# Linear attention and gated MLP on one core: which transfers SyncE waits for before the program ends

## The chip, the core and the metric

The kernel runs on one core of a Trainium2 chip. The core has five instruction streams: TensorE (PE) multiplies matrices, VectorE (DVE) and ScalarE (ACT) work on elements, GpSimd (POOL) does small set-up work and issues accumulating transfers, and SyncE (SP) computes nothing: here it issues nearly all DMA transfers and waits for semaphores. A semaphore is a counter that an instruction or a finished transfer raises; a wait holds an engine's own stream until the counter has reached a value.

The metric is the device time of one execution in microseconds; the median over the timed runs counts. Beside them stands one profiled execution. Its "span" runs from the first to the last instruction that the profile has of the program.

## The reference

`x` is 2048 x 1024, in bf16. It is normalised per row, and the result `xn` goes two ways: through linear attention with 32 heads (A), and through a gated MLP with 3584 inner columns (B). The output joins them.

```python
xn = _layernorm(x, axis=-1)
# A: qkv = xn @ wqkv, per head of 32 columns
pq, pk = phi(q), phi(k)                  # phi(t) = where(t > 0, t + 1, exp(t)) + 1e-6
kv  = einsum("bhsd,bhse->bhde", pk, v);  z = sum of pk over s
o   = einsum("bhqd,bhde->bhqe", pq, kv) / (einsum("bhqd,bhd->bhq", pq, z) + 1e-6)
s   = o @ wo
# B
g   = _silu((silu(xn @ w_gate) * (xn @ w_up)) @ w_down)
return x + s * g
```

## The kernel before

**Tiling and stages.** The large products are made block-wise with seven partial products for each 2 x 2 blocks in place of eight (class `Set`), with sums and differences of blocks formed by VectorE and ScalarE; some of the seven are split once more in the same way (class `Joint`). The stages are: normalise `x` and transpose it; K and V and their sums over rows; gate, up and Q for column blocks of 512; the attention output `s`, which goes to a scratch tensor in DRAM (`s_scr`); at the end the product with `w_down`.

**The last stage.** It runs over four groups `g` of 512 rows (class `Group`). The function `evac` inside `Group.dset` finishes a piece of the output: ScalarE takes the silu of a finished PSUM bank, VectorE multiplies it with the piece of `s`. In groups 0 to 2, GpSimd adds the piece to the output in DRAM by an accumulating transfer (helper `dacc`, L374). In group 3, VectorE adds `x`, which was loaded for it, and SyncE stores the piece (helper `dma`, L370). The semaphores of these stores are named `d_oo`, then the number of the buffer for `x` (0 to 7), then the first column. Buffer 7 is stored in three pieces, of 256, 128 and 128 columns (`PIECES`), so there are ten of them, and each is raised by one transfer.

**What sets the order.** Every operation is recorded by `Plan.op` with the tile regions that it reads and writes. From those regions `op` works out `preds`, the earlier operations that it must wait for, and `succs`, the later ones that must wait for it. `Plan.schedule` simulates the five streams and settles one order for each; the list `BOOST` of hand-set preferences bears on it. `Plan.emit` walks that order and writes, for each engine, a list of entries `("w", semaphore, value)` for a wait and `("i", function, semaphore, increment)` for an operation. A wait is left out where the engine knows already, by an earlier wait of its own or through the engine it waited for, that the semaphore has reached the value. `o.ev` holds an operation's semaphore, the key of it, the value that it reaches with the operation, and what the engine knew by then. `PL.count` holds each semaphore's final value. `_run` (L219) plays an engine's list: L222 is `wait_ge`, the next lines the operation.

**The end of the program.** After `emit`, waits are appended to SyncE's list. They stand behind its last store, and no operation of SyncE follows them. Then SyncE leaves its block by a branch and takes part in the barrier of all engines that ends the program (both have the line L254 in the profile). The compiler puts up to two waits into one semaphore instruction, and the last wait into the branch.

Of the kernel before, what the change touches and what calls it, by code (L numbers as in the profile page):

```python
# [240 lines left out]
def build_kernel(nc, A_x, A_wqkv, A_wo, B_w_gate, B_w_up, B_w_down, out, WINDOW=10, NWARM=13, NPE=4, LEAD=16.0, CLAMP=1000.0, AHEAD=4.0):  # L241
# [12 lines left out]
    with ExitStack() as es:  # L254
# [76 lines left out]
        semn = {}  # L331
# [6 lines left out]
        PL = Plan(WINDOW, LEAD, CLAMP, AHEAD)  # L338
# [1300 lines left out]
        sp = {}  # L1639
# [99 lines left out]
            PL.ops[k].boost = v  # L1739
        PL.schedule()  # L1740
        prog = PL.emit(esem)
        for s in semn.values():
            if id(s) in PL.count:
                prog["sp"].append(("w", s, PL.count[id(s)]))

        @block.tensor
        def _(h):
# [19 lines left out]
def bass_recurrent_scan__linear_attn_block__swiglu_ffn__prompt_kernel(  # L1767
    nc: bass.Bass,
    A_x: bass.AP,
    A_wqkv: bass.AP,  # L1770
    A_wo: bass.AP,
    B_x: bass.AP,
    B_w_gate: bass.AP,
    B_w_up: bass.AP,
    B_w_down: bass.AP,
    out: bass.AP,
):
    build_kernel(nc, A_x, A_wqkv, A_wo, B_w_gate, B_w_up, B_w_down, out)
# [28 lines left out]
```

## Time and profile before

| | before |
|---|---|
| timed runs, median (lowest to highest) | 705.55 us (705.12 to 705.91), 3 runs |
| profiled execution, its own time | 704.51 us |
| span of the profiled execution | 702.7 us |
| granted TensorE clock, mean | 0.998 |
| last matmul ends | 696.75 us |
| SyncE's semaphore instructions of L222: all / from 698 us on | 69 / 59 |

In the rows that follow, "start us, us" are the start from the beginning of the span and the time that it took. SPq, POOLq and so on are instructions of an engine's sequencer alone (waits, barriers, branches, DMA issues); the profile doesn't count them as busy, and the chain of waits doesn't run through them unless something counted was released. In the views by source line, "x59: 17/28/28, 698.4 to 702.2" is the count, the shortest, median and longest duration in ns, and the first and last start. A row that begins with two times and a colon is a stage of the table by stage: it has the length, the busy time of PE, PEld, DVE, ACT and POOL, the granted clock, the mean busy share of the 16 DMA engines and GB/s. A row "DMA" with 40 digits has the busy share of the DMA engines in tenths, in 40 equal slices of the stretch. In a row of a DMA issue the last number is the time from issue to landing.

### The profile page before, as it was taken

Reading aid. Unit: us, or ns where it says so; the run is one execution under the profiler, and the core shown is the slowest. Engines: PE = TensorE matmul, PEld = TensorE weight load, DVE = VectorE, ACT = ScalarE, POOL = GpSimd, SP = SyncE. Lnnn points to the kernel's source line nnn. Section 1 sums busy time; section 2 is a strip of 40 time slices with the busy share of each in tenths; the row PEclk is TensorE's granted clock in tenths of the full one; section 3 lists DMA queues with packets and bytes.
Section 4 is the critical chain, followed back from the end, with each engine's and each line's share of the span. In section 5 each row is a group of like instructions: output and inputs, shape, how many; then the busy total and the mean of one; then the engine's idle time right before and its main releaser. Section 6 shows DMA issues by size and latency. Waiting matters only on the chain.

```text
span 702.7 us, 11996 instructions
## 1 busy us (share of the span) xinstructions
PE 694.8 (99%) x4436; PEld 421.4 (60%) x4436; DVE 610.7 (87%) x1391; ACT 424.7 (60%) x848; POOL 68.4 (10%) x87
## 2 busy tenths in 40 slices
PE   8999999999999999999999999999999999999996
PEld 3544445555555566666666666666665448687784
DVE  6999998667999799898999999888879998768685
ACT  4877645867978967868866567775763113232222
POOL 2111000001100011020110110001101211111010
PEclk9999999999999999999999999999999999999999
DMA  9434213126612376584670486766627875666672
GB/s 313 106 83 106 54 60 121 61 90 145 155 61 69 117 195 169 174 236 101 166 194 1 106 242 198 242 218 165 165 81 225 192 182 176 155 165 156 207 180 69
DMA packets 96107, 103.68 MB, mean 148 GB/s; under 512 B 18256, under 2 KB 91344, under 8 KB 95952
## 3 DMA queue, kind: packets, MB, share of 16 engines
q1 hardware_dynamic: 84976, 92.43, 41.9%
q0 software_dynamic: 11072, 10.49, 11.9%
q8 instruction: 35, 0.57, 0.3%
q14 instruction: 24, 0.20, 0.1%
HBM read 65.54 MB, written 37.36 MB: 146 GB/s over the span
## 4 chain that ended last, share of the span: by engine, by line
PE 99%; ACT 0%; POOL 0%; DVE 0%; issue 0%; POOLq 0%
PE ps L230 99%; PE ps L237 0%; ACT X L358 0%; DVE W L368 0%; POOL TM L415 0%; ACT W L358 0%; POOL TM L414 0%; POOLq L1792 0%
## 5 line engine op out<-in xcount | busy, mean ns | idle before, releaser
L358 ACT ACTIVATE TM<-ps 128x512 f32<-128x512 f32 (+2 forms) x341 | 169.0, 528 | 50.5 <-PE ps L230 45.6
L368 DVE TENSOR_TENSOR ps<-ps,TM 128x256 f32<-128x256 f32 (+1 forms) x322 | 157.7, 509 | 40.2 <-PE ps L230 35.8
L230 PE MATMUL ps<-X,W 128*128 128x512 f16 (+1 forms) x896 | 190.4, 340 | 0.0
L230 PE MATMUL ps<-P,W 128*128 128x512 f16 (+1 forms) x896 | 188.9, 338 | 0.0
L358 ACT ACTIVATE H<-ps 128x512 f16<-128x512 f32 (+1 forms) x181 | 106.3, 601 | 55.9 <-PE ps L230 54.9
L230 PEld LDWEIGHTS ps<-X,W 128*128 128x128 f16 (+1 forms) x896 | 87.5, 98 | 59.5 <-DVE W L368 0.2
L230 PEld LDWEIGHTS ps<-P,W 128*128 128x128 f16 (+1 forms) x896 | 87.6, 98 | 58.4 <-DVE ps L368 0.2
L358 ACT ACTIVATE ps<-ps 128x256 f32<-128x256 f32 (+2 forms) x149 | 63.5, 426 | 72.5 <-PE ps L230 70.9
L230 PE MATMUL ps<-H,X 128*128 128x512 bf16 (+4 forms) x556 | 104.8, 336 | 0.5 <-ACT X L358 0.5
L368 DVE TENSOR_TENSOR H<-H 128x1024 f16<-128x1024 f16 (+5 forms) x150 | 87.1, 598 | 10.6 <-ACT H L358 8.4
L368 DVE TENSOR_TENSOR W<-W 128x256 f16<-128x256 bf16 (+6 forms) x256 | 89.1, 388 | 5.1 <-PE ps L230 2.9
L230 PE MATMUL ps<-W 128*128 128x256 f16 x512 | 90.0, 273 | 0.0
L368 DVE TENSOR_TENSOR TM<-ps,TM 128x512 f32<-128x512 f32 x99 | 67.8, 686 | 12.5 <-PE ps L230 11.5
L230 PEld LDWEIGHTS ps<-H,X 128*128 128x128 f16 x556 | 52.8, 98 | 41.6 <-ACT X L358 0.6
L375 POOL DMA_DIRECT2D h_scratch<-H x28 | 33.7, 1283 | 437.4 <-DVE H L368 197.0
L230 PEld LDWEIGHTS ps<-W 128*128 128x128 f16 (+1 forms) x512 | 50.0, 98 | 27.3 <-ACT TM L358 0.6
L230 PE MATMUL ps<-H,W 128*128 128x512 f16 (+2 forms) x280 | 63.6, 358 | 0.0
L230 PE MATMUL ps<-H 128*128 128x256 f16 (+4 forms) x432 | 60.9, 273 | 0.0
L230 PE MATMUL ps<-W,H 128*128 128x256 f16 (+1 forms) x314 | 53.5, 305 | 0.0
L358 ACT ACTIVATE H<-TM 128x512 f16<-128x512 f32 x61 | 38.3, 631 | 15.6 <-DVE TM L368 15.0
L230 PEld LDWEIGHTS ps<-H 128*128 128x128 f16 (+1 forms) x432 | 38.3, 98 | 14.6 <-ACT H L358 0.2
L368 DVE TENSOR_TENSOR H<-ps,TM 128x512 f16<-128x512 f32 (+1 forms) x59 | 40.3, 685 | 2.7 <-PE ps L230 2.5
(92 smaller groups left out, 552.1 us busy)
## 6 DMA issues: line engine op xcount, KB each, us to landing
h_scratch<-H SPq DMA_DIRECT2D x70, 256.0 KB, 3.2
X<-h_scratch SPq DMA_DIRECT2D x15, 896.0 KB, 5.2
W<-in_B_w_gate_dram SPq DMA_DIRECT2D x7, 1024.0 KB, 5.4
W<-in_B_w_up_dram SPq DMA_DIRECT2D x7, 1024.0 KB, 6.1
h_scratch<-H POOLq DMA_DIRECT2D x28, 256.0 KB, 5.7
H<-in_B_w_down_dram SPq DMA_DIRECT2D x8, 896.0 KB, 6.7
W<-in_A_x_dram SPq DMA_DIRECT2D x16, 256.0 KB, 3.1
H<-in_A_wqkv_dram SPq DMA_DIRECT2D x8, 512.0 KB, 7.9
```

The costliest lines, as they stand in the source:

```text
L230: last = h.matmul(o, l, r, start=st, stop=sp, skip_group_check=True)
L358: op = PL.op("act", reads, writes, lambda h: h.activation(o, i, func, **kw), nel(o) / 1200.0 + (0.055 if src == "ps" else 0.095))
L368: return dve(reads, writes, lambda h: h.tensor_tensor(o, a, b, op), nel(o), 1.92 if fast else 0.96)
L375: return PL.op("pool", reads, writes, lambda h: h.dma_start(o, i, accum_op=ALU.add), 1.0, sem=s, nbytes=2 * nbytes)
```

## The change

Before, SyncE waits at the end for the final value of every semaphore that any transfer raises: 118 of them. The change goes over the operations in scheduled order and, for each transfer that no later operation depends on (`o.succs` is empty), notes its semaphore with the value that it reaches with that transfer; a later transfer on the same semaphore takes the place of the earlier. Only these are waited for.

```diff
         PL.schedule()
         prog = PL.emit(esem)
-        for s in semn.values():
-            if id(s) in PL.count:
-                prog["sp"].append(("w", s, PL.count[id(s)]))
+        ends = {}
+        for o in PL.order:
+            if o.sem is not None and not o.succs:
+                ends.pop(id(o.sem), None)
+                ends[id(o.sem)] = o.ev
+        for s, _, val, _ in ends.values():
+            prog["sp"].append(("w", s, val))
```

The ten that are left are the stores of group 3. Their order in the list changes too: it is that of the stores now.

The only place where the instructions differ is the end of SyncE's stream. The rows are SyncE's last two stores and the branch out of its block, with the semaphores waited for ahead of it (the row of before is cut off by the view; `s_dve` is VectorE's own semaphore, the `d_` names are those of transfers).

```order
@@ -223,3 +223,3 @@
 L371 DMA out_dram<-W 128x256 [waits s_dve]
 L371 DMA out_dram<-W 128x128 [waits s_dve] x2
-L254 UNCONDITIONAL_BRANCH [waits d_so3,d_so4,d_so2,d_so5,d_so1,d_so6,d_so0,d_so7,d_ha4_1,d_so8,d_hs6_1,d_wdR010,d_hs6_0,d_wdR011,d_ha4_0,d_wdR110,d_ha0_1,d_wdR111,d_hs2_1,d_wdR000,d_hs2_0,d_wdR001,d_ha0_0,d_wdR100,d_rr1_3,d_wdR101,d_rr1_2,
+L254 UNCONDITIONAL_BRANCH [waits d_oo4_0,d_oo6_0,d_oo5_0,d_oo7_0,d_oo2_0,d_oo7_256,d_oo3_0,d_oo7_384,d_oo1_0,d_oo0_0]
```

Nothing ahead of the branch has moved, on SyncE or on the other engines, but for line numbers.

## The prediction

> **What bounds the kernel now.** I read the page first, then the chain of waits in order of time near the end, then the last microseconds stage by stage, and last the waiting instructions themselves, by source line. The page and the end of the chain:
>
> ```profile
> PE 694.8 (99%) x4436; PEld 421.4 (60%) x4436; DVE 610.7 (87%) x1391; ACT 424.7 (60%) x848; POOL 68.4 (10%) x87
> ...
> 679.91 16.84 PE ps L230 x125
> 696.75 0.02 issue
> 696.77 0.28 ACT W L358
> 697.06 0.02 issue
> 697.08 0.24 DVE W L368
> 697.32 0.02 issue
> 697.34 0.23 DVE W L368
> ```
>
> TensorE is busy for 99% of the span, and the chain is TensorE's until 696.75 us; two short evacuations follow, on ScalarE and VectorE. The chain stops there, at 697.57, because the profile does not count semaphore and DMA-issuing instructions as work. The span is 702.7 us, so 5.1 us lie behind the last arithmetic. Nothing of this change stands earlier than that, and these 5.1 us have a limit of their own. The timeline of SyncE, the table by stage, and the transfers from 697.8 us on (40 slices of 0.13 us) show who is at work in them:
>
> ```profile
> 691.41 6.89 SPq L371 DMA_DIRECT2D out_dram<-W  x7
> ...
> 698.30:699.40 1.10, 0.00 (x0) 0.00 (x0) 0.00 (x0) 0.00 (x0) 0.00 (x0) 1.00 0.27 60
> 699.40:702.30 2.90, 0.00 (x0) 0.00 (x0) 0.00 (x0) 0.00 (x0) 0.00 (x0) 0.54 0.01 3
> 702.30:702.70 0.40, 0.00 (x0) 0.00 (x0) 0.00 (x0) 0.00 (x0) 0.00 (x0) 0.50 0.00 0
> ...
> DMA  3940740181000000000000000002000000000000
> q1 hardware_dynamic: 438, 0.14, 10.4%
> q14 instruction: 1, 0.01, 0.6%
> ```
>
> SyncE issues its last store until 691.41 + 6.89 = 698.30. From then on no engine computes (five times 0.00). Up to 699.4 the stores still move, 60 GB/s; from 699.4 to 702.3 the DMA engines are 1% busy. The row of slices says the same: data until the tenth slice, 699.1 us, and one lone digit at slice 28, which starts at 701.3 us and must be the only packet that is not of queue q1, an instruction fetch. So for 2.9 us neither an engine nor a store is busy. What runs is SyncE's list of waits (the helper at L222 issues them):
>
> ```profile
> L222 SPq EVENT_SEMAPHORE  x59: 17/28/28, 698.4 to 702.2; - x59
> ...
> L222 SPq EVENT_SEMAPHORE  x17: 28/28/28, 699.0 to 700.0; - x17
> ...
> L222 SPq EVENT_SEMAPHORE  x1: 28/28/28, 700.4 to 700.4; - x1
> L222 SPq EVENT_SEMAPHORE  x4: 28/28/28, 700.8 to 701.0; - x4
> ...
> L254 SPq COMPARE_BRANCH  x1: 41/41/41, 702.3 to 702.3; - x1
> L254 SPq DRAIN  x1: 7/7/7, 702.5 to 702.5; - x1
> L254 POOLq EVENT_SEMAPHORE  x2: 17/17/17, 702.5 to 702.6; - x2
> ```
>
> The first row is the whole list: 59 instructions, the first at 698.4, the last at 702.2, none longer than 28 ns, so none of them stood waiting. The second is the list between 699 and 700 us: 17 in a microsecond, 0.06 us each. The next two are the list from 700.4 to 700.7 and from 700.7 to 701: there is one pause, from 700.4 to 700.8, some 0.3 us longer than a step. Check: 58 steps of 0.06 plus 0.3 is 3.8 us, as from 698.4 to 702.2. The last rows are the way out: a branch at 702.3, SyncE's drain, the barrier through GpSimd (its own end comes at 702.7). **The end of the program is set by the number of instructions in this list.**
>
> **The change part by part.** It takes 108 of 118 semaphores out of that list. Two semaphores fit one instruction (59 instructions and the branch, with two in 58 of them, carry 118); ten take five instructions and the branch. So 54 of SyncE's instructions go. No other engine's work, no transfer and no order changes; SyncE's last issue stays at 698.30.
>
> *What is removed.* 54 x 0.06 = 3.2 us, plus the pause of 0.3 us, if it belongs to the long list: 3.5 us. By instructions alone the list would end at 698.4 + 5 x 0.06 = 698.7.
>
> *What is late next.* The ten that stay are the output stores themselves, and the last of these is still under way then. The two last stores, and the time from their issue to their landing:
>
> ```profile
> L371 SPq DMA_DIRECT2D out_dram<-W x2: 430/431/432, 697.4 to 697.9; - x2
> DMA to landing us min/median/max: 1.5/1.5/1.5
> ...
> out_dram<-W SPq DMA_DIRECT2D x1, 64.0 KB, 2.0
> out_dram<-W SPq DMA_DIRECT2D x2, 32.0 KB, 1.5
> ```
>
> The last store, 32 KB, is issued at 697.9 and lands 1.5 us later, at 699.4. The one before it lands at 697.4 + 1.5 = 698.9 and the 64 KB one before that 2.0 us after its issue, which is still earlier than 699.4. So of the four real waits only the last counts. It takes back 699.4 - 698.7 = 0.7 us of the 3.5; under those 0.7 us the five remaining wait instructions cost nothing. Without that cover (a landing at once) they would cost 0.3 us. That a SyncE instruction which really waits starts late after the landing is not seen in this list. I bound it below by nothing and above by one step of the list, 0.06 us, and take nothing.
>
> *What stays.* From the last wait (702.2) to the end (702.7): 0.5 us, unchanged.
>
> *The sum.* 699.4 + 0.5 = 699.9 us against 702.7: **2.8 us less in the span.** The profiled execution took 704.5 us, 1.8 us more than its span; I leave those 1.8 us as they are, since they lie outside the program: 701.7 for a profiled run. The median of the timed runs, 705.55, is 1.0 us over the profiled execution, with a spread of 705.1 to 705.9. The difference is taken over: 705.55 - 2.8 = **702.7 us**.
>
> *Bounds.* The landing is the one term that can move: 1.5 us here, 2.0 us for the 64 KB store; the longest for a store of the last stage is this:
>
> ```profile
> L371 SPq DMA_DIRECT2D out_dram<-W x8: 332/332/600, 685.8 to 696.8; - x8
> ...
> DMA to landing us min/median/max: 1.7/1.7/3.0
> ```
>
> With 2.0 for the last store the gain is 2.3 us (703.2), with 3.0 it is 1.3 (704.2). I take 1.5, since it belongs to both stores of that very size at that very place. On the other side a landing of 1.4 with rounding in favour gives 2.9 to 3.0.
>
> **The rivals.**
>
> *Instruction fetch.* A list that is 54 instructions shorter moves every place where SyncE's stream goes on to the next block of instructions. The profile shows one such place: the pause at 700.4, and 0.9 to 1.0 us behind it the fetch of q14, which lasts 0.6% x 16 engines x 5.2 us = 0.5 us. In before that fetch was for instructions that were needed later, so only 0.3 us of it showed. That place is (702.3 - 700.8) / 0.06 = 25 instructions before the branch; with 54 fewer it is 29 behind the branch, in the closing code. If the code behind it is not on hand, SyncE stands for 1.0 + 0.5 = 1.5 us: 2.8 - 1.5 leaves 1.3, 704.3 us. The Trainium skill, Runtime: NRT & Kernel Launch, in Instruction fetch mechanics, speaks for this rival: a taken branch to a target outside the two pages on hand forces a fetch before execution can go on. Against it stand the branch at 702.3 and the drain at 702.5 in before: 0.2 us in all, no room for a fetch, and what follows the branch follows it in the stream too. 3%, for one or two such fetches (two: 705.8).
>
> *Slower.* The same mechanism, in series: the place is the way out behind the branch at L254, the price 1.5 us for each block that has to be fetched with SyncE standing, and every other engine held by the barrier. It decides from the third block on: 3 x 1.5 - 2.8 = 1.7 us lost, 707.2 us. For it speaks only that the border between two blocks moves into the closing code; against it, that the one crossing the trace shows cost 0.3 us and not 1.5. 3%.
>
> *The list is faster without the profiler.* The step of 0.06 us is seen while each instruction is recorded. Elsewhere recorded instructions start closer together, four on GpSimd at the very start:
>
> ```profile
> 0.30 0.10 POOL L1792 MEMSET const-float32-0.0<- 128x1 f32 x1 [0.30 <-issue]
> 0.34 0.10 POOL L1792 MEMSET const-float32-1.0<- 128x1 f32 x1
> 0.37 0.10 POOL L1792 MEMSET const-bfloat16-1.0<- 128x1 bf16 x1
> 0.41 0.10 POOL L1792 MEMSET const-uint8-127<- 128x1 uint8 x1
> ```
>
> (0.41 - 0.30) / 3 = 0.037 us. If that were the step in a timed run, the list of before would end at 698.4 + 59 x 0.037 = 700.6 instead of 702.2, and the change would be worth 700.6 - 699.4 = 1.2 us: 704.4 us. Against it: the recording does not hold the engines to 0.06, as these very rows show, so the step is rather that of the instruction; and the profiled execution was not the slower one. 4%.
>
> *It does nothing.* Something else could set the end, in the 1.8 us outside the span or by a transfer that a dropped wait was really for. The 1% of the DMA engines from 699.4 on, which is the fetch alone, rules out the transfer; a fixed time outside can't be seen from here. 705.5 us, 3%.
>
> **How the numbers follow.** The forecast holds 87%, and the predicted time is its own: 702.7. Its bounds are the landing (2.3 to 2.9 us of gain, 702.6 to 703.2) and the scatter of a median, for which I take the 0.4 us by which the runs of before differ from theirs: 702.2 to 703.6. I widen that by a little at both ends, to **702.1 to 703.9**, for a landing between 2.0 and 3.0 us; the four rivals, 13%, stay outside. 0.2% of the time is 1.4 us; that is about what a measurement of this kernel tells from no change. The forecast is a gain of 2.8 us or 0.4%, so its 87% go to faster. The single or double fetch (3%), the faster list (4%) and no effect (3%) end within 0.2%: 10%. The fetches in series go to slower: 3%.
>
> **What would show it.** Right: in the changed kernel's profile the L222 rows of SyncE behind 698 us fall from 59 to 5 and the last of them starts at 699.4, at the landing of the last store; the branch follows within 0.1 us and the span ends 0.5 us after the landing, at 699.9; no pause is in the list, and the row of slices has no stretch of zeros before the end but the last half microsecond. The chain up to 697.57 is unchanged. Wrong: a gap of a microsecond or more between branch and drain with a q14 packet in it (fetch); a last landing well beyond 1.5 us after its issue (the landing mis-sized); a span that falls by 2.8 while the timed median falls by 1.2 or less (the list faster without the profiler, or a fixed end outside the span).

## The result, and the profile after

| | before | with the change |
|---|---|---|
| timed side by side, median (lowest to highest) | 705.25 us (704.91 to 705.91), 6 runs | 701.84 us (701.15 to 703.17), 6 runs |
| profiled execution, own time | 704.51 us | 701.97 us |
| span of it | 702.7 us | 700.3 us |

The ratio is 0.9954, with a 95% interval of 0.9942 to 0.9966: 3.4 us or 0.5% faster, by the interval 2.4 to 4.1 us. The prediction was faster, 702.7 us, in a range of 702.1 to 703.9. The sign and the mechanism came out; the time lies 0.3 us below the range.

In the changed kernel's profile the end of the chain of waits reads (start us, us, what):

```profile
690.53 6.84 PE ps L230 x62
697.37 0.02 issue
697.39 0.29 ACT W L358
697.68 0.02 issue
697.71 0.24 DVE W L368
697.94 0.02 issue
697.97 0.22 DVE W L368
```

The links are those of before, but each is 0.6 us later (697.97 in place of 697.34). The change can't do that; where it comes from is told below. Behind it, the views by source line once more: the waits, the last store, the way out.

```profile
L222 SPq EVENT_SEMAPHORE  x5: 17/28/28, 698.7 to 699.8; - x5
...
L371 SPq DMA_DIRECT2D out_dram<-W x1: 433/433/433, 698.2 to 698.2; - x1
DMA to landing us min/median/max: 1.5/1.5/1.5
...
L254 SPq COMPARE_BRANCH  x1: 41/41/41, 699.9 to 699.9; - x1
L254 SPq DRAIN  x1: 7/7/7, 700.0 to 700.0; - x1
```

And the table by stage for the same stretch (from, to and length, then five engines' busy time, the granted clock, the DMA engines' share and GB/s):

```profile
699.10:699.80 0.70, 0.00 (x0) 0.00 (x0) 0.00 (x0) 0.00 (x0) 0.00 (x0) 1.00 0.21 47
699.80:700.30 0.50, 0.00 (x0) 0.00 (x0) 0.00 (x0) 0.00 (x0) 0.00 (x0) 0.95 0.00 0
```

The 59 wait instructions are 5. The last store is issued at 698.2 and lands 1.5 us later, at 699.8 (698.23 + 1.55 by its unrounded times); the last wait starts then, the branch 0.1 us behind it, and the span ends 0.5 us after the landing. Stores move until 699.8, and only the last half microsecond is empty. From the start of the last issue to the end it is 700.3 - 698.2 = **2.0 us**, in before 702.7 - 697.9 = **4.8 us**. (By the unrounded times 2.02 and 4.83.) The difference is the 2.8 us of the prediction. The clock times that it named for the landing and the end, 699.4 and 699.9, came at 699.8 and 700.3. The span fell by only 2.4: the 0.6 us by which the chain came later count against the 2.8, and the last issue, which followed VectorE's last result 0.27 us closer than in before, counts for it. The timed medians fell by 3.4. So the question for the experiments was whether the change is worth 2.8 us and the rest is scatter (theory A), or some 0.6 us more that does not lie in the tail (theory B).

### The profile page after: what moved, and what is told of

It reads as the page before. It is cut to its first block, busy times and chain, and to the rows that moved or that the text cites. A ratio compares the mean times of both kernels' runs of the same rounds, so it can differ in the third digit from the quotient of the medians.

```text
span 700.3 us, 11921 instructions
## 1 busy us (share of the span) xinstructions
PE 694.2 (99%) x4415; PEld 421.7 (60%) x4436; DVE 610.9 (87%) x1391; ACT 424.7 (61%) x848; POOL 68.5 (10%) x87
## 4 chain that ended last, share of the span: by engine, by line
PE 98%; DMA 1%; SPq 0%; issue 0%; ACT 0%; DVE 0%
PE ps L230 98%; DMA H<-in_A_wqkv_dram 1%; PE ps L237 0%; SPq L371 0%; ACT H L358 0%; ACT ps L358 0%; DVE W L368 0%; ACT W L358 0%
## 5 line engine op out<-in xcount | busy, mean ns | idle before, releaser
L230 PE MATMUL ps<-H,X 128*128 128x512 bf16 (+4 forms) x545 | 103.1, 335 | 1.2 <-ACT X L358 0.5
```

Source lines behind the costliest of these rows:

```text
L230: last = h.matmul(o, l, r, start=st, stop=sp, skip_group_check=True)
```

## The experiments

### The size: both kernels again

No edit; twice the kernel before, twice the changed one.

> The kernel before, with no edit, timed against itself: what it shows is the scatter of the comparison. Theory A (the change is worth the 2.8 us of the tail and the rest of the measured 3.4 us is scatter): ratio 1.000, its interval about as wide as that of the change (0.2%), and a profiled span that differs from 702.7 us by up to 1 us, with all of the difference in the first 10 us. Theory B (the shorter program is worth some 0.6 us more, outside the tail): ratio 1.000 as well, but an interval clearly under 0.1%, so that 0.6 us can't be scatter.

> The changed kernel once more, with more runs. Theory A: 2.8 us less than before, ratio 0.9960; the time from the start of the last store's issue to the end is 2.0 us again. Theory B: 3.4 us less, ratio 0.9952, with the same 2.0 us of tail.

> The changed kernel a third time, five rounds, to settle the size beside the 3.4 and 2.6 us measured so far. Theory A (2.8 us of tail, the rest scatter): 2.8 us by the medians within 0.5 us, and a tail of 2.0 us in the trace. Theory B (0.6 us more outside the tail): 3.4 us again.

> The kernel before, unedited, beside it. Both theories: ratio 1.000. In the trace: tail 4.8 us, and any difference of the span from 702.7 us made up of the start (up to about 27 us) and of the time that SyncE takes to issue the 64 KB store, with VectorE's work between them as long as in the other traces to 0.01 us.

| | time | before, beside it | difference | ratio, 95% interval | tail in its trace |
|---|---|---|---|---|---|
| before again | 704.95 us (11 runs) | 705.08 us (15) | -0.1 us | 0.9995, 0.9987 to 1.0004 | 4.8 us |
| change again | 702.53 us (5) | 705.08 us (15) | -2.6 us | 0.9962, 0.9950 to 0.9975 | 2.0 us |
| before, third | 705.02 us (11) | 704.98 us (15) | 0.0 us | 1.0003, 0.9994 to 1.0011 | 4.8 us |
| change, third | 702.27 us (5) | 704.98 us (15) | -2.7 us | 0.9963, 0.9950 to 0.9977 | 2.0 us |

Theory A's 2.8 us are met twice within 0.3, theory B's 3.4 us not again, though the interval of each of the two comparisons alone (1.8 to 3.5 us and 1.6 to 3.5 us) just holds it. Before against itself is no different, in an interval 0.17% wide, where theory A had about 0.2% and theory B clearly under 0.1%: half a microsecond can be scatter in such a comparison. Two more facts speak against theory B. In every timed run whose span is on record, of before and of the change, the time is 1.67 to 1.87 us more than the span, and its mean is the same 1.7 to 1.8 in both, so the gain doesn't lie outside the span. Inside it, the traces of the change don't start earlier: the operation on `veps` shown below begins at 26.55 to 27.22 us in its three traces and at 26.60 to 27.20 in the three of before. One thing is mixed in: the comparisons ran on different chips. Before's median was 705.08 us on the chip of the first repeat and 704.98 on that of the second; the chip of the comparison with 3.4 us is not on record.

Where the scatter comes from can be read in the traces. VectorE's small operation on `veps` is the same instruction of the program in each, and so are its last two operations; for before, the change, the kernel with 24 waits put back (below) and the third trace of before:

```profile
26.60 0.14 DVE L746 TENSOR_SCALAR veps<-mv 128x1 f32<-128x1 f32 x1
697.08 0.48 DVE L368 TENSOR_TENSOR W<-W 128x128 f16<-128x128 f16 x2 [0.22 <-ACT W L358]
```

```profile
27.22 0.15 DVE L746 TENSOR_SCALAR veps<-mv 128x1 f32<-128x1 f32 x1
697.71 0.48 DVE L368 TENSOR_TENSOR W<-W 128x128 f16<-128x128 f16 x2 [0.22 <-ACT W L358]
```

```profile
27.93 0.14 DVE L746 TENSOR_SCALAR veps<-mv 128x1 f32<-128x1 f32 x1
698.41 0.48 DVE L368 TENSOR_TENSOR W<-W 128x128 f16<-128x128 f16 x2 [0.22 <-ACT W L358]
```

```profile
27.20 0.15 DVE L746 TENSOR_SCALAR veps<-mv 128x1 f32<-128x1 f32 x1
697.68 0.49 DVE L368 TENSOR_TENSOR W<-W 128x128 f16<-128x128 f16 x2 [0.22 <-ACT W L358]
```

697.08 - 26.60, 697.71 - 27.22, 698.41 - 27.93 and 697.68 - 27.20 are 670.48 or 670.49 us, and so it is in all twelve traces. The whole body runs the same to 0.01 us. What differs is how late the first 27 us leave it, by 1.3 us between the first and the third trace. The second place is SyncE's issues of the last stores. By source line, the 64 KB store in before and in the change, and in the third trace of before the one ahead of it and the last two:

```profile
L371 SPq DMA_DIRECT2D out_dram<-W x1: 600/600/600, 696.8 to 696.8; - x1
```

```profile
L371 SPq DMA_DIRECT2D out_dram<-W x1: 334/334/334, 697.4 to 697.4; - x1
```

```profile
L371 SPq DMA_DIRECT2D out_dram<-W x1: 1611/1611/1611, 696.6 to 696.6; - x1
...
L371 SPq DMA_DIRECT2D out_dram<-W x2: 430/438/445, 698.7 to 699.2; - x2
```

The issue held SyncE for 0.60 us, for 0.33, and in the third for 1.61 (there it is the 128 KB store, not the one that the expectation names). In that trace the last store went out at 699.2, 1.0 us after VectorE's last result at 697.68 + 0.49, instead of 0.3. The two together make the whole difference between the two spans of before: 0.60 us at the start and 0.73 us at the end, 704.0 - 702.7 = 1.3. In the trace of before again the span is 703.4 us, 0.7 more than in before, and 0.4 of that is the longer issue of the 64 KB store (1.03 us); so the expectation that all of the difference lies in the first 10 us missed.

### The dropped waits at another place

```diff
+        dead = [("w", s, PL.count[id(s)]) for s in semn.values() if id(s) in PL.count and id(s) not in ends]
+        stores = {id(o.fn) for o in PL.order if o.sem is not None and id(o.sem) in ends}
+        at = max(n for n, e in enumerate(prog["sp"]) if e[0] == "i" and id(e[1]) not in stores) + 1
+        prog["sp"][at:at] = dead
         for s, _, val, _ in ends.values():
             prog["sp"].append(("w", s, val))
```

> All 118 waits are kept, and SyncE's stream is as long as before (364 instructions); the 108 for transfers that something else waits for stand ahead of SyncE's last eight stores, where SyncE is idle. Theory A: the place counts, not the number; tail 2.0 us as in the change, gain 2.8 us, ratio 0.9960. Theory B (the length of the program counts): the tail is 2.0 us but the gain stays 0.6 us behind that of the change run beside it. A third possibility: the 3.5 us of waits delay the first of the eight stores enough to push the last one, then the last issue is up to 1 us later than VectorE's last result.

```profile
687.31 0.43 SPq L371 DMA_DIRECT2D W<-in_A_x_dram  x1
691.44 7.13 SPq L371 DMA_DIRECT2D out_dram<-W  x8
```

```profile
L222 SPq EVENT_SEMAPHORE  x54: 27/28/28, 687.8 to 691.4; - x54
L222 SPq EVENT_SEMAPHORE  x5: 17/28/28, 698.6 to 699.7; - x5
...
L371 SPq DMA_DIRECT2D out_dram<-W x2: 430/430/430, 697.7 to 698.1; - x2
```

These are SyncE's timeline and, by source line, its waits, early and late, and the last two stores. The 54 instructions are all there and take their 3.6 us, from 687.8 to 691.4, with the pause among them. They hold back the first of the eight stores, and the last one is not pushed by that: it is issued at 698.1, 0.22 us behind VectorE's last result, and the tail is 2.02 us by the unrounded times. 702.02 us beside 705.08, 3.1 us less, ratio 0.9960 (0.9946 to 0.9974). The number of waits and the length of the program are as before, and the gain does not stay behind that of the change beside it (2.6 us): it is the place behind the last store that costs.

### The list doubled

```diff
         for s in semn.values():
             if id(s) in PL.count:
                 prog["sp"].append(("w", s, PL.count[id(s)]))
+        for s in semn.values():
+            if id(s) in PL.count:
+                prog["sp"].append(("w", s, PL.count[id(s)]))
```

> The list of 118 waits stands twice at the end, in 118 instructions instead of 59. Theory A: 59 x 0.06 = 3.5 us more than before in the profiled tail (8.3 us from the last store's issue to the end instead of 4.8), and the same 3.5 us in the timed runs, ratio 1.0050. Rival (the list is faster when it is not recorded, 0.037 us an instruction): 3.5 us in the trace but only 2.2 us in the timed runs, ratio 1.0031.

709.65 us beside 705.08, ratio 1.0062 (1.0049 to 1.0074): 4.6 us more by the medians, 3.5 to 5.2 by the interval, where theory A had 3.5 and its rival 2.2. The waits, in three stretches (the whole list, up to 700.05, from 700.06 on), and the last two stores:

```profile
L222 SPq EVENT_SEMAPHORE  x118: 17/28/1034, 699.0 to 707.4; - x118
L222 SPq EVENT_SEMAPHORE  x2: 17/526/1034, 699.0 to 699.0; - x2
L222 SPq EVENT_SEMAPHORE  x116: 27/28/28, 700.1 to 707.4; - x116
...
L371 SPq DMA_DIRECT2D out_dram<-W x2: 430/431/432, 698.0 to 698.5; - x2
DMA to landing us min/median/max: 1.5/1.5/1.5
```

The compiler sorts the pairs in another way for the longer list, and the second instruction now waits for the last store. It stands for 1.03 us, until that store lands at 698.5 + 1.5 = 700.0, and only then the other 116 begin, at 0.06 us each. In before the trace has the wait for the last store in the last of the 59 instructions, at 702.2, so that the landing and the list ran beside each other. 3.5 us for 59 more instructions and 1.03 us for that cover lost are the 4.6 us; the expectation missed the second term. The trace's tail, 707.9 - 698.5 = 9.4 against 4.8, says 4.6 as well, and so the timed runs follow the 0.06 us of the trace, not the 0.037 of the rival, which with the same second term would give 3.2. But a span is on record for each of the timed runs too, so what a run does of which nothing is recorded stays open.

### As many waits as fit under the landing

```diff
+        dead = [("w", s, PL.count[id(s)]) for s in semn.values() if id(s) in PL.count and id(s) not in ends][:24]
+        prog["sp"] += dead
         for s, _, val, _ in ends.values():
             prog["sp"].append(("w", s, val))
```

> 24 of the 108 dropped waits are put back ahead of the ten: 17 semaphore instructions on SyncE behind the last store instead of 5. Theory (the end is the later of the list, 0.06 us an instruction from 0.5 us after the last issue began, and the landing, 1.5 us after it): 0.5 + 16 x 0.06 = 1.5 us, so the list just fits under the landing: from the start of the last issue to the end 2.0 us, at most 2.1. Rival (each wait instruction has a price wherever it stands): 2.0 + 12 x 0.06 = 2.7 us.

```profile
L222 SPq EVENT_SEMAPHORE  x17: 17/28/28, 699.4 to 700.5; - x17
...
L371 SPq DMA_DIRECT2D out_dram<-W x2: 430/430/430, 698.5 to 698.9; - x2
DMA to landing us min/median/max: 1.5/1.5/1.5
L254 SPq COMPARE_BRANCH  x1: 41/41/41, 700.6 to 700.6; - x1
```

17 wait instructions, the last at 700.5, the landing of the last store (698.9 + 1.5). The span ends at 701.0, 2.0 us after the last issue began (2.03 by the unrounded times), as with 5 instructions and not 2.7 as by the rival: twelve more of them cost nothing here. (Its one time, 702.68 us, says little: this is the trace with the latest start.)

### The border of a block at the exit

The same edit with 56 in place of 24.

> 56 of the dropped waits are put back: 33 semaphore instructions, so that SyncE's 335th profiled instruction, ahead of which before paused for 0.3 us, is no wait but the drain behind the closing branch. Theory (a pause of 0.3 us at the border of a block, wherever it lies): the list ends 0.5 + 33 x 0.06 = 2.5 us after the last issue began, the branch there, the pause between branch and drain, end at 2.5 + 0.4 + 0.3 = 3.2 us. Fetch rival of the prediction (a block behind the branch is fetched with SyncE standing, 1.5 us): 4.4 us. If the border costs nothing: 2.9 us.

```profile
L222 SPq EVENT_SEMAPHORE  x33: 17/28/28, 698.2 to 700.2; - x33
...
L254 SPq COMPARE_BRANCH  x1: 41/41/41, 700.3 to 700.3; - x1
L254 SPq DRAIN  x1: 79/79/79, 700.7 to 700.7; - x1
...
L371 SPq DMA_DIRECT2D out_dram<-W x2: 430/430/430, 697.3 to 697.8; - x2
```

And its transfers from 700 to 701.1 us:

```profile
DMA packets 0, 0.00 MB, mean 0 GB/s; under 512 B 0, under 2 KB 0, under 8 KB 0
```

The list is without a pause; the pause now lies between the branch and the drain, 0.4 to 0.5 us apart instead of 0.2, and no fetch stands in it: its packet comes at 701.4, behind the end of the span. The last store was issued at 697.8, the span ends at 701.0, 3.3 us later by the unrounded times: 3.2 was expected, 4.4 by the fetch rival, 2.9 if the border costs nothing. The pause belongs to a place in SyncE's stream (ahead of the 336th of SyncE's rows, in the traces of before and of this kernel alike; the expectation has it as the 335th) and costs 0.3 to 0.4 us wherever that place meets the critical path. What SyncE does in it is not shown. One time, 702.85 us.

### Stores on ScalarE's queue

```diff
+                    if c0 == 256:
+                        PL.op("act", [xr], [], lambda h: h.dma_start(of[row:row + 128, cols], xa), 0.08,
+                              sem=dsem("oo%d_%d" % (x.k, c0)), nbytes=n * 128)
+                        return
                     dma([xr], [], of[row:row + 128, cols], xa, dsem("oo%d_%d" % (x.k, c0)), n * 128)
```

and for the second kernel `c0 == 384`.

> The changed kernel, with the store of the middle piece (columns 256 to 383 of the last tile) issued by ScalarE instead of SyncE. In the traces so far SyncE's issue of the 64 KB store ahead of it took 0.33 to 1.03 us, and the last store was issued 0.04 to 0.74 us after VectorE's last result. Theory: the last store then waits only for VectorE and for the rest of that one issue: 0.04 to 0.2 us after the result, 0.3 us less than the change beside it on average, ratio to before 0.9956. Rival: ScalarE's first store of the program is issued or lands later than SyncE's, and is now the last to land: no gain, or a loss of up to 1 us against the change.

> The changed kernel, with the store of the last piece (columns 384 to 511) issued by ScalarE, which has nothing else to do by then. Theory: it is issued 0.05 us after VectorE's last result whatever SyncE's issues take; 0.3 us less than the change on average, ratio to before 0.9956, and the middle store or this one is the last to land. Rival: as for the middle store; ScalarE's issue takes longer or its transfer lands more than 1.5 us after its issue, and the gain is used up.

702.15 us and 701.95 us, beside 704.67 for before (9 runs): ratios 0.9961 (0.9949 to 0.9974) and 0.9960 (0.9947 to 0.9974), that is 2.5 and 2.7 us. Neither is told apart from the change. In the first kernel's trace, SyncE's two stores and ScalarE's one:

```profile
L371 SPq DMA_DIRECT2D out_dram<-W x2: 432/890/1349, 697.0 to 698.4; - x2
DMA to landing us min/median/max: 1.7/2.3/2.9
...
L1600 ACTq DMA_DIRECT2D out_dram<-W x1: 378/378/378, 697.2 to 697.2; - x1
DMA to landing us min/median/max: 2.6/2.6/2.6
```

ScalarE issued the middle store at once, at 697.2, but it took 2.6 us to land, and SyncE's issue of the 64 KB store beside it took 1.35 us, so that the last store left at 698.4, 0.58 us behind VectorE's last result; theory had at most 0.2. In the second kernel the 64 KB issue took 0.92 us (917 ns in the row below) and the other store on SyncE followed it late, at 698.2. ScalarE's own was issued 0.03 us behind VectorE's last result, as theory had it, and landed first:

```profile
L371 SPq DMA_DIRECT2D out_dram<-W x2: 431/674/917, 697.2 to 698.2; - x2
DMA to landing us min/median/max: 1.8/2.1/2.3
...
L1600 ACTq DMA_DIRECT2D out_dram<-W x1: 400/400/400, 698.1 to 698.1; - x1
DMA to landing us min/median/max: 1.7/1.7/1.7
```

So a second queue doesn't shorten this end by what these runs can tell. No run tried what lengthens SyncE's issue, but the kept traces point at an instruction fetch. In all twelve, one packet of 16 KB on queue q8 starts while the sixth of group 3's ten stores (128 KB) is under way. In the first kernel here, between 696 and 698.4 us, and in the one with 24 waits put back, between 697 and 698.5:

```profile
q8 instruction: 1, 0.02, 4.5%
```

```profile
q8 instruction: 1, 0.02, 3.7%
```

As shares of 16 engines' time these are 1.7 and 0.9 us, the longest of the twelve and nearly the shortest. The sixth store lands 1.0 to 1.2 us after that packet ends: 3.7 us after its issue in the first kernel here, 2.7 in the other, where the five stores of 128 KB ahead of it take 1.7 to 1.8. In each of the eight traces in which a later issue held SyncE for over 0.5 us, it let go 0.37 to 0.40 us after the packet's end. This is an agreement in time; no experiment moved the packet.

## Why the prediction was right or wrong

**What bounds the end: right.** It was the number of wait instructions behind the last store. They were taken away, moved, doubled and put back in two amounts, and each time the tail followed the count at 0.06 us an instruction or the landing, whichever was later (2.0, 2.0, 9.4, 2.0, 3.3 us), once the place of the one real wait in the list and the pause are counted in.

**What is removed, what is late next, what stays: right.** The terms, against their measurement in the changed kernel: landing 1.5 us after its issue, forecast 1.5; last wait to the end 0.5, forecast 0.5; a real wait starts 0.02 us after its landing by the unrounded times (bounded by nothing and 0.06, taken as nothing); the tail 2.8 us shorter, forecast 2.8. That the store's landing takes back 0.7 us of the 3.5 is borne out by the kernel with 24 waits put back, in which those 0.7 us hold twelve more instructions for nothing.

**The rivals.** Fetch at the exit and fetches in series fell by the changed kernel itself, whose drain follows the branch as closely as before, and by the kernel with the border placed there: 0.3 to 0.4 us, no packet. "It does nothing" fell with the result. The faster list without recording finds no support in the timed runs, with the reserve above.

**The time and the range: wrong.** The steps that failed are two numbers taken from three runs: the base, in "705.55 - 2.8" at the end of "The sum", and the scatter, in "the 0.4 us by which the runs of before differ from theirs" in "How the numbers follow". The measured 701.84 lies 0.9 us below 702.7. Of this 0.3 is the base, since before itself came at 705.25 beside the change, and 0.6 is the gain, 3.4 in place of 2.8.
- The base was high. Over the 45 runs of before that stood beside the change or an experiment (6, 15, 9 and 15), its median is 704.98 us, 0.6 under 705.55. With that base the same gain gives 702.2.
- The scatter was taken too small. The three runs lay within 0.8 us; the 45 of before lie between 704.08 and 706.45, and the change's own six cover 2.0 us. Its 16 runs from three comparisons have a median of 702.37 us and a mean of 702.27, from 701.15 to 703.17; the medians of the three are 701.84, 702.53 and 702.27, and the first lies 0.5 below that of all. Against the 45 runs of before (mean 705.04) the difference is 2.6 us by the medians and 2.8 by the means.

So of the 3.4 us of the first comparison 2.8 are the tail. The other 0.6 are put down to scatter: nothing in the later runs asks for theory B, but only one of those six runs left a trace, so where the 0.6 lay in them is not shown. The prediction's sentence that the profiled execution differs from the median by 1.0 us, "taken over", should have been the warning: 704.51 was a run with an early start, and a kernel whose own runs differ by 1 us does so with any change in it. What delays the start by up to 1.3 us in its first 27 us, while the first loads arrive, was not tried.

## What to carry to other kernels

A wait that is already satisfied is cheap but not free: 0.06 us an instruction here, which counts in full where nothing else runs, behind the last store. Wait there for what can still be under way and let dependences cover the rest, or put the other waits where the engine idles; and a list that is shorter than the last landing costs nothing. When a forecast is a few tenths of a per cent, take the base from many runs and the range from their scatter: the gain in the tail was known to 0.1 us from the trace, the time was not known to 0.5.

## What the runs showed that was not expected

- The body of this kernel, 670 us long, takes the same time to 0.01 us in all twelve traces; but for the waits themselves, the differences between them arise in the first 27 us and in the issues and landings of the last stores.
- The same store's issue on SyncE takes between 0.33 and 1.35 us, and the one ahead of it once 1.61 us; where it is long, it ends 0.4 us behind an instruction fetch that ran while the stores were under way. A 32 KB store from ScalarE's queue landed once after 2.6 us, in the trace with the longest such fetch, and once after 1.7, where those on SyncE take 1.5 to 1.8.
- A pause of 0.3 us stands at a fixed place of SyncE's stream: it moves with the number of instructions ahead of it, from the list (before) to the early waits (the dropped waits at another place) and to the way out (56 put back), and is gone from the changed kernel's span, which ends ahead of it.
